# One fixed list of steps, laid out anew: the recurrent-attention and feed-forward kernel in another order

## The chip, the cores and the metric

The kernel runs on one core of a Trainium2 chip. The metric is the device time of one execution in microseconds (us). Three executions of the kernel before took 522.6, 523.03 and 520.49 us: median 522.6.

## What is computed

The reference runs a gated linear recurrence over 768 positions for 4 batches and 8 heads of width 48, and puts its output through a two-matrix feed-forward block with a squared ReLU.

```python
for t in range(S):                                   # S = 768, state is (B, H, D, D)
    cur = einsum('bhd,bhe->bhde', u * k[t], v[t])
    y[:, :, t] = einsum('bhd,bhde->bhe', r[t], state + cur)
    state = w[t][..., None] * state + einsum('bhd,bhe->bhde', k[t], v[t])
x = y.transpose(0, 2, 1, 3).reshape(3072, 384)
h = maximum(x @ w_in, 0)                             # w_in 384 x 2048
out = (h * h) @ w_out                                # w_out 2048 x 384
```

The two weight matrices come in 8-byte floats. Everything else is 4-byte.

## The kernel before

**Tiling.** The 768 positions are cut into 6 chunks of 128. For each chunk there are four attention units, one per batch (`attention`, lines 456 to 813), and then the feed-forward block on the chunk's 512 tokens (`ffn`, line 849). In chunk 0 the first six of sixteen feature blocks are done on batches 0 and 1 and then again on batches 2 and 3 (256 columns each); from the seventh on, 512 columns at once. Feature block pairs share a piece of weights, so there are 8 pieces of `w_in` (`ri`, `wi`) and 8 of `w_out` (`ro`, `wo`).

**A unit of chunk 0.** Six loads bring w, r and k of two batches (SP, line 471) and four more the v of one (line 504). PE transposes w, k and r (step "turn", line 518, four matmuls each). DVE scans w along time (line 535, four instructions), ScalarE takes Ln and Exp of it (lines 542 and 543), DVE makes the scaled k (lines 558, 559, 562). PE forms the scores ("mt", line 756), DVE masks them (759), PE mixes them with v (line 780, "mix" and "mix2") and makes the new state ("dS", line 790), which DVE scales (line 812). ACT and DVE move the result out as a high and a low part (lines 611 and 614). From chunk 1 on, the score, state and mixing matmuls of neighbouring units stand in one step (lines 650, 668, 677, 687).

**A feature block.** Nine matmuls into a PSUM bank `hp` ("hp", line 860; two banks), ReLU and square and a copy on ACT (lines 865, 867, 871), the low part on DVE ("g4", line 872), then per batch three matmuls into `ob` ("ob", line 878; four banks).

**Weights.** An 8-byte piece is made into two 4-byte parts by six steps: ACT (line 428), DVE (lines 432, 436, 441), ACT (448) and one subtraction on POOL (449).

**What sets the order.** Nothing is scheduled when the kernel is built. The 2,446 steps are made in a fixed way and numbered; the table `ORDER` says in which order they are issued, `PLACES` which buffer of its pool each of 549 tile lifetimes gets, and `FILLS` before which steps PE runs dummy matmuls. Every engine and the DMA queue of SP work in that order, each strictly one after the other:

```python
for n in order:                      # Plan.order, line 72
    s = self.steps[n]
    ...
        place = pool[places[self.slots[k]]] if places else ...
...
for s in self.order():               # Plan.run, line 91
    if self.filler and s.fill[0]:
        self.filler(*s.fill)
    s.fn()
...
for _ in range(count):               # fill, line 350
    T.matmul(to, ident, ident, is_transpose=True, ...)
```

A filler is one 128 x 128 transpose of the identity (line 351) into a part of a PSUM bank that nobody reads. It waits for nothing but its place in PE's order.

Of the kernel before, what the change touches and what calls it, by code (L numbers as in the profile page):

```python
# [96 lines left out]
class Names:  # L97
# [121 lines left out]
)  # L219
FILLS = {  # L220
    16: (2, 'ob', 1), 55: (6, 'ob', 3), 30: (3, 'ob', 1), 57: (4, 'ob', 1), 71: (2, 'ob', 0), 48: (5, 'ob', 1), 82: (3, 'ob', 3), 89: (5, 'ob', 1),
    145: (3, 'ob', 0), 144: (7, 'ob', 0), 127: (8, 'side', 0), 168: (4, 'side', 0),
}

# [794 lines left out]
```

## Time and profile before

| | |
|---|---|
| profiled execution | 521.4 us, span 519.7 us |
| median of three executions | 522.6 us |
| PE busy | 506.6 us, 97% of the span |
| VectorE (DVE) busy | 358.3 us, 69% |
| ScalarE (ACT) busy | 319.1 us, 61% |
| GpSimd (POOL) busy | 87.8 us, 17% |
| SP's DMA queue | 46.82 MB, 47.6% of 16 engines' span |
| granted TensorE clock, mean | 1.0 |

A share of busy time is a mean over stages with different limits, so the stages are read one by one. The span is what the profiler saw from the first to the last instruction; the time of the execution is 1.7 us more. A matmul's end is modelled, and matmuls overlap, so start times say more than durations.

### The profile page before, as it was taken

How to read it: one execution, taken by the hardware profiler on the slowest of the kernel's cores; microseconds unless marked ns; L12 is line 12 of the kernel's file. 1: busy time of each engine (PE TensorE's matmuls, PEld its weight loads, DVE VectorE, ACT ScalarE, POOL GpSimd, SP SyncE). 2: the span in 40 equal slices, each digit the busy share in tenths (PEclk: the TensorE clock that was granted, in tenths of full speed). 3: DMA queues.
4: the chain of work that ended last, by engine and by line, in shares of the span. 5: the costliest groups of instructions: out<-in, count | busy, mean ns of one | idle time of the engine just before them, and what ended most of it. 6: DMA issues, size and time to landing. Idle time of an engine off the chain costs nothing.

```text
span 519.7 us, 13752 instructions
## 1 busy us (share of the span) xinstructions
PE 506.6 (97%) x5452; PEld 458.5 (88%) x5452; DVE 358.3 (69%) x787; ACT 319.1 (61%) x878; POOL 87.8 (17%) x133
## 2 busy tenths in 40 slices
PE   8999999999999999999998999999999999999996
PEld 7888898888999998899987989889988888998895
DVE  6999789898687988768778658678476354333332
ACT  4999898996766867666573656564543363433232
POOL 3025233344021040212203001303000000000000
PEclk9999999999999999999999999999999999999999
DMA  7999977363847765575772480661181000100001
GB/s 152 225 165 247 246 151 205 88 92 63 148 71 100 147 97 95 106 125 73 117 129 37 84 137 15 112 122 36 32 133 32 3 19 6 59 16 0 1 2 65
DMA packets 188310, 48.74 MB, mean 94 GB/s; under 512 B 178000, under 2 KB 183120, under 8 KB 188240
## 3 DMA queue, kind: packets, MB, share of 16 engines
q1 hardware_dynamic: 187520, 46.82, 47.6%
q8 instruction: 45, 0.74, 0.6%
q10 hardware_dynamic: 720, 0.98, 0.5%
q14 instruction: 25, 0.20, 0.1%
HBM read 31.65 MB, written 4.72 MB: 70 GB/s over the span
## 4 chain that ended last, share of the span: by engine, by line
PE 78%; SPq 5%; issue 5%; DVE 4%; ACT 4%; DMA 2%; POOL 1%; POOLq 0%; ACTq 0%; DVEq 0%
PE ob L878 35%; PE hp L860 34%; PE ob L668 2%; SPq L504 2%; PE ob L687 2%; DMA ri<-in_moe_w_in_dram 2%; PE a L677 2%; SPq L415 1%; PE a L650 1%; PE hp L635 1%; SPq L471 1%; POOL wi L449 1%; DVE pt L535 1%; ACT t L865 1%; DVE m L550 1%
## 5 line engine op out<-in xcount | busy, mean ns | idle before, releaser
L878 PE MATMUL ob<-wo,g 128*128 128x384 f32 x1152 | 227.0, 340 | 0.1
L860 PE MATMUL hp<-x,wi 128*128 128x512 f32 (+1 forms) x1062 | 221.8, 355 | 3.2 <-DVE g L872 2.5
L878 PEld LDWEIGHTS ob<-wo,g 128*128 128x128 f32 x1152 | 199.4, 188 | 8.1 <-DVE g L872 0.9
L860 PEld LDWEIGHTS hp<-x,wi 128*128 128x128 f32 x1062 | 174.1, 188 | 29.7 <-DVE g L872 3.7
L869 DVE SCALAR_TENSOR_TENSOR hp<-hp,t 128x512 f32<-128x512 f32 (+1 forms) x96 | 58.2, 606 | 74.5 <-ACT t L865 74.2
L865 ACT ACTIVATE t<-hp 128x512 f32<-128x512 f32 (+1 forms) x118 | 61.0, 517 | 72.2 <-PE hp L860 47.7
L872 DVE TENSOR_TENSOR g<-hp,g 128x512 fp32r<-128x512 f32 (+1 forms) x118 | 69.1, 587 | 35.5 <-ACT g L871 35.0
L871 ACT CAST g<-hp 128x512 fp32r<-128x512 f32 (+1 forms) x118 | 59.6, 506 | 49.5 <-DVE hp L869 48.6
L630 ACT ACTIVATE m<-diag,beta 128x64 f32<-128x64 f32 x160 | 40.4, 338 | 3.4 <-DVE beta L593 3.3
L658 POOL MEMSET S<- 1x1 f32 x20 | 2.2, 110 | 237.4 <-PE ob L668 237.4
L614 DVE SCALAR_TENSOR_TENSOR x<-ob,x 112x128 fp32r<-112x128 f32 x80 | 21.2, 284 | 19.3 <-ACT x L611 16.5
L822 ACT COPY ob<-zero 112x128 f32<-112x128 f32 x80 | 20.7, 270 | 17.3 <-PE ob L878 10.1
L611 ACT ACTIVATE x<-ob 112x128 fp32r<-112x128 f32 x80 | 19.1, 275 | 17.3 <-PE ob L687 12.1
L535 DVE TENSOR_TENSOR_SCAN pt<-pt,zero 112x128 f32<-112x128 f32 x64 | 27.2, 456 | 2.4 <-DMA x<-x 1.1
L449 POOL TENSOR_TENSOR wi<-q,wi 128x768 fp32r<-128x768 f32 x8 | 17.1, 2135 | 55.1 <-ACT wi L448 44.0
L584 POOL TENSOR_TENSOR st<-st 128x384 f32<-128x384 f32 x16 | 16.7, 1043 | 33.0 <-DVE st L480 32.5
L480 DVE STREAM_TRANSPOSE st<-st 128x1152 f32<-128x1152 f32 x16 | 21.6, 1363 | 0.0
L542 ACT ACTIVATE m<-pt 112x512 f32<-112x512 f32 x24 | 15.1, 631 | 9.2 <-DVE pt L535 8.2
L449 POOL TENSOR_TENSOR wo<-q,wo 128x768 fp32r<-128x768 f32 x8 | 15.9, 1983 | 18.1 <-ACT wo L448 14.8
L558 DVE TENSOR_TENSOR pt<-pt,m 112x512 f32<-112x512 f32 x24 | 16.9, 706 | 2.4 <-ACT Ec L557 1.3
L559 DVE SCALAR_TENSOR_TENSOR m<-pt,m 112x512 f32<-112x512 f32 x24 | 18.0, 748 | 0.3
L709 DVE COPY_PREDICATED m<-caus,a 128x256 f32<-128x256 uint8 x40 | 17.3, 439 | 0.9 <-PE a L650 0.9
(125 smaller groups left out, 540.0 us busy)
## 6 DMA issues: line engine op xcount, KB each, us to landing
pt<-st SPq DMA_DIRECT2D x96, 96.0 KB, 2.9
ro<-in_moe_w_out_dram SPq DMA_DIRECT2D x8, 768.0 KB, 6.1
v<-in_v_dram SPq DMA_DIRECT2D x96, 48.0 KB, 2.8
out_dram<-q SPq DMA_DIRECT2D x20, 192.0 KB, 2.1
ri<-in_moe_w_in_dram SPq DMA_DIRECT2D x32, 96.0 KB, 4.9
ri<-in_moe_w_in_dram SPq DMA_DIRECT2D x8, 384.0 KB, 6.1
st<-in_r_dram SPq DMA_DIRECT2D x8, 384.0 KB, 5.3
st<-in_w_dram SPq DMA_DIRECT2D x8, 384.0 KB, 4.9
```

Source lines behind the costliest of these rows:

```text
L449: P.add("pool", 1.9, rank(8 * k + 5), lambda q=q, tt=tt: G.tensor_tensor(out=tt[:, 1], in0=q.tile, in1=tt[:, 0].bitcast(F32), op=ALU.subtr ...
L480: V.transpose(out=zt[:, i].rearrange("a t p q i -> a t (p q) i"), in_=sv[:, :, i].rearrange("s t p q x -> s t (p q) x"))
L535: lambda p=p: V.tensor_tensor_scan(out=pt[:, 0, p], data0=src(0)[:, p], data1=zero.broadcast_to([HP, C]), initial=1.0, op0=ALU.mult, op1=A ...
L614: made.append(P.add("dve", c2, rank(nm + "l"), lambda y=y, hi=hi, lo=lo: V.scalar_tensor_tensor(out=lo(), in0=y(), scalar=-1.0, in1=hi().b ...
L630: A.activation(M.tile[:, o:o + Q], diag2, AF.Copy, scale=beta.tile[:, i:i + 1])
L822: P.add("act", 0.16, rank("zero"), lambda p=p: A.copy(out=obs[p][0:HP, DM:], in_=zero[0:HP].broadcast_to([HP, C])), w=[("YO", p)], after=t ...
L860: T.matmul(hp.tile[:, 0:n], wi[f][:, wl, kt], xT[:, kt, xl, xs], start=(m == 0), stop=(m == 3 * KT - 1))
L865: P.add("act", 0.49 if full else 0.28, rank("g1"), lambda: A.activation(t(), h(), AF.Relu), r=[hp], w=[(g, 1)])
L869: P.add("dve", 0.605 if full else 0.337, rank("g2"), lambda: V.scalar_tensor_tensor(out=h(), in0=h(), scalar=0.0, in1=t(), op0=ALU.max, op ...
L871: P.add("act", 0.48 if full else 0.26, rank("g3"), lambda: A.copy(out=hi(), in_=h()), r=[hp], w=[(g, 0)])
L872: P.add("dve", 0.605 if full else 0.335, rank("g4"), lambda: V.tensor_tensor(out=lo(), in0=h(), in1=hi().bitcast(F32), op=ALU.subtract), r ...
L878: T.matmul(obs[b][:, 0:DM], g.tile[0][:, gl, o:o + C], wo[f][:, wl], start=(f == 0 and m == 0), stop=(f == NF - 1 and m == 2))
```

## The change

The steps, their instructions and their buffers' sizes stay. `ORDER`, `PLACES` and `FILLS` are replaced in part. Places 817 to 2445 of `ORDER` are as before; of the first 817, nearly all hold another step. On PE the last differing place is the 165th step of 593, "hp at 40.0", which the trace of before has at 148.6 us; from there on every engine has the same steps in the same order. There are 68 fillers in place of 52, before twelve steps as before, of which five are others.

```diff
 ORDER = (
-    4, 14, 17, 19, 6, 16, 0, 5, 20, 1, 18, 26, 15, 11, 7, 23, 24, 25, 55, 58, 309, 21, 22, 27, 28, 8, 2, 13, 30, 9, 57, 31, 312, 59, 33, 56, 64, 10, 29, 61,
...
+    4, 6, 14, 19, 20, 16, 11, 18, 51, 0, 1, 17, 5, 23, 12, 15, 9, 2, 26, 21, 22, 309, 7, 311, 310, 57, 8, 64, 312, 10, 24, 25, 27, 28, 30, 31, 32, 29, 33, 55,
...
 FILLS = {
-    16: (2, 'ob', 1), 55: (6, 'ob', 3), 30: (3, 'ob', 1), 57: (4, 'ob', 1), 71: (2, 'ob', 0), 48: (5, 'ob', 1), 82: (3, 'ob', 3), 89: (5, 'ob', 1),
-    145: (3, 'ob', 0), 144: (7, 'ob', 0), 127: (8, 'side', 0), 168: (4, 'side', 0),
+    16: (2, 'ob', 1), 1: (4, 'ob', 2), 15: (2, 'ob', 2), 57: (4, 'ob', 1), 56: (9, 'ob', 1), 71: (2, 'ob', 0), 48: (11, 'ob', 1), 89: (8, 'ob', 1),
+    144: (13, 'ob', 0), 127: (2, 'ob', 0), 473: (9, 'side', 0), 191: (2, 'side', 0),
 }
```

What this does to the engines is shown at three places. A line that begins with - stood there before, with + stands there now.

**The start.** In SP's queue, from the sixth transfer of before (the eighth now). `st_143` holds w, k and r of batches 0 and 1 of chunk 0, `v_91` the v of batch 0, `ri_56` the first piece of `w_in`:

```order
 L415 DMA ri_56<-in_moe_w_in_dram 48x512
-L471 DMA st_143<-in_k_dram 128x8x48
-L504 DMA v_91<-in_v_dram 64x4x48
-L471 DMA st_143<-in_r_dram 128x8x48
+L471 DMA st_143<-in_w_dram 128x8x48
 L415 DMA ri_56<-in_moe_w_in_dram 16x3x512
+L415 DMA ri_56<-in_moe_w_in_dram 48x512
+L471 DMA st_143<-in_k_dram 128x8x48
```

The k of batch 1 was the seventh transfer and is now the twelfth. On PE the same stretch, from the transpose of batch 0's k to that of batch 1's k; `ob_147` to `ob_150` are the four `ob` banks, `hp_151` and `hp_152` the two `hp` banks:

```order
+L351 MATMUL ob_149<-ident 128x128 x2
 L518 MATMUL ob_149<-ident,st_143 112x128 x4
-L351 MATMUL ob_150<-ident 128x128 x6
-L518 MATMUL ob_150<-ident,st_143 112x128 x4
-L351 MATMUL ob_148<-ident 128x128 x3
-L575 MATMUL ob_147<-ut,m_162 128x4 x4
 L351 MATMUL ob_148<-ident 128x128 x4
 L518 MATMUL hp_152<-ident,st_143 112x128 x4
+L575 MATMUL ob_147<-ut,m_163 128x4 x4
+L518 MATMUL ob_150<-ident,st_143 112x128 x4
+L351 MATMUL ob_148<-ident 128x128 x9
 L518 MATMUL hp_151<-ident,st_143 112x128 x4
```

Batch 1 is transposed in the order r, w, k in place of w, r, k, and nine fillers now stand ahead of its k. The step behind this piece is the scores of batch 0.

**The last batch of chunk 0.** On PE, the transposes of batch 3 (`st_144`) and the scores of batch 2 (L756, into `a_153` and `a_154`, the two PSUM banks of pool `a`):

```order
 L860 MATMUL hp_151<-x_142,wi_57 128x256 x9
-L351 MATMUL ob_147<-ident 128x128 x3
 L518 MATMUL a_154<-ident,st_144 112x128 x4
-L351 MATMUL ob_147<-ident 128x128 x7
+L351 MATMUL ob_147<-ident 128x128 x13
 L518 MATMUL ob_149<-ident,st_144 112x128 x4
-L518 MATMUL hp_152<-ident,st_143 112x128 x4
 L756 MATMUL a_153<-pt_136 64x128
```

The second feature block, which stood ahead of this piece, now stands behind the scores that begin at its last row, and so does the first transpose of chunk 1 (`st_143`). Thirteen fillers stand between the two transposes where there were seven, with three more ahead.

**Feature blocks and weights.** On DVE, the low parts of the last half-width block and of the first full-width one (L872, 128x256 and 128x512) among the steps on the weights (`q`, lines 432 to 441). Before:

```order
L872 TENSOR_TENSOR g_99<-hp_151,g_99 128x256
L436 SCALAR_TENSOR_TENSOR q_156<-ro_70,q_156 128x768
L812 TENSOR_TENSOR S_140<-a_154,Ec_172 112x96
L441 SCALAR_TENSOR_TENSOR q_156<-ro_70,q_156 128x768
L872 TENSOR_TENSOR g_95<-hp_152,g_95 128x512
```

Now:

```order
L436 SCALAR_TENSOR_TENSOR q_156<-ro_70,q_156 128x768
L441 SCALAR_TENSOR_TENSOR q_156<-ro_70,q_156 128x768
L872 TENSOR_TENSOR g_99<-hp_152,g_99 128x256
L558 TENSOR_TENSOR pt_135<-pt_135,m_166 112x512
L872 TENSOR_TENSOR g_95<-hp_151,g_95 128x512
```

Two weight operations stood between the two low parts and now stand ahead of both. In SP's queue of the same stretch a transfer of the seventh piece of `w_in` (`ri_80`), whose place holds v of chunk 0, has come ahead of the second halves of the sixth and fourth pieces (`ro_78`, `ro_70`):

```order
L415 DMA ri_80<-in_moe_w_in_dram 16x3x512
L504 DMA v_160<-in_v_dram 64x4x48
L417 DMA ro_78<-in_moe_w_out_dram 128x2x768
L417 DMA ro_70<-in_moe_w_out_dram 128x2x768
L415 DMA ri_76<-in_moe_w_in_dram 96x2x512
```

Before, `ro_70` went out ahead of every transfer of `ri_80`, and `ro_78` behind some of them.

## Rows read from the trace of the kernel before

**Rows 1.** The profile's page: busy us (share of the span) and instructions.

```profile
PE 506.6 (97%) x5452; PEld 458.5 (88%) x5452; DVE 358.3 (69%) x787; ACT 319.1 (61%) x878; POOL 87.8 (17%) x133
```

**Rows 2.** Busy by stretch: us, PE, PEld, DVE, ACT, POOL, PEclk, DMA share, GB/s.

```profile
5.58:57.00 51.42, 48.26 (x645) 42.88 (x645) 45.13 (x87) 44.16 (x124) 13.92 (x7) 1.00 0.94 210
33.00:57.00 24.00, 22.52 (x288) 19.94 (x285) 21.42 (x37) 22.12 (x59) 9.48 (x5) 1.00 0.93 223
57.00:80.00 23.00, 22.04 (x171) 20.56 (x171) 19.29 (x31) 20.78 (x49) 6.46 (x4) 1.00 0.88 186
80.00:150.00 70.00, 69.93 (x820) 63.02 (x819) 59.64 (x124) 59.02 (x165) 21.10 (x20) 1.00 0.58 116
150.00:300.00 150.00, 147.85 (x1906) 135.97 (x1905) 118.71 (x287) 95.96 (x295) 30.22 (x52) 1.00 0.60 99
```

**Rows 3.** PE in order of time: start, us, line, operation, [idle before].

```profile
12.96 0.90 PE L756 MATMUL a<-pt 64*64 64x128 f32 x32
...
31.66 0.93 PE L351 MATMUL ob<-ident 128*128 128x128 f32 x7
32.42 0.60 PE L518 MATMUL ob<-ident,st 128*112 128x128 f32 x4
...
33.39 0.90 PE L756 MATMUL a<-pt 64*64 64x128 f32 x32
...
53.31 0.65 PE L518 MATMUL hp<-ident,st 128*112 128x128 f32 x4 [0.87 <-DVE g L872]
...
57.56 1.35 PE L860 MATMUL hp<-x,wi 128*128 128x256 f32 x9
```

**Rows 4.** All fillers (line 351): count, ns least/mean/most, first and last start.

```profile
L351 PE MATMUL ob<-ident x52: 270/273/421, 6.4 to 47.3; 128*128 128x128 f32 x52
```

**Rows 5.** SP's queue: the twelfth transfer; landing times of line 471, 0 to 16 us.

```profile
9.92 0.60 SPq L471 DMA_DIRECT2D st<-in_w_dram  x1
...
DMA to landing us min/median/max: 3.2/4.2/5.0
```

**Rows 6.** DVE in order of time: scans, batch 2's scaled k, two weight operations.

```profile
26.71 0.73 DVE L535 TENSOR_TENSOR_SCAN pt<-ob,zero 112x128 f32<-112x128 f32 x2
...
30.90 0.26 DVE L812 TENSOR_TENSOR S<-a,Ec 112x96 f32<-112x96 f32 x1
31.07 0.69 DVE L562 TENSOR_TENSOR pt<-ob,m 112x512 f32<-112x512 f32 x1
...
49.46 0.96 DVE L436 SCALAR_TENSOR_TENSOR q<-ro,q 128x768 uint32<-128x768 uint32 x1
...
50.46 2.47 DVE L441 SCALAR_TENSOR_TENSOR q<-ro,q 128x768 uint32<-128x768 uint32 x1
```

**Rows 7.** Two subtractions on POOL in order of time; ACT's group of line 605.

```profile
39.91 2.70 POOL L449 TENSOR_TENSOR wi<-q,wi 128x768 fp32r<-128x768 f32 x1 [6.52 <-ACT wi L448]
...
49.75 2.36 POOL L449 TENSOR_TENSOR wo<-q,wo 128x768 fp32r<-128x768 f32 x1 [2.11 <-ACT wo L448]
...
L605 ACT ACTIVATE st<-st,nfar 128x384 f32<-128x384 f32 x24 | 14.8, 619 | 0.2
```

**Rows 8.** POOL, DVE and PE in order of time, 74 to 81 us.

```profile
74.78 1.84 POOL L449 TENSOR_TENSOR wi<-q,wi 128x768 fp32r<-128x768 f32 x1 [6.75 <-ACT wi L448]
74.94 2.49 DVE L436 SCALAR_TENSOR_TENSOR q<-ro,q 128x768 uint32<-128x768 uint32 x1
...
79.13 2.13 PE L860 MATMUL hp<-x,wi 128*128 128x512 f32 x8 [0.96 <-DVE g L872]
```

**Rows 9.** Whom PE waited for, 150 to 300 us: total, times, longest.

```profile
PE hp L860 <- DVE g L872: 1.5, 1, 1.5
```

**Rows 10.** Line 417's landing times; batch 3's state on PE; ACT's weight step.

```profile
DMA to landing us min/median/max: 4.8/6.1/10.1
...
56.95 0.67 PE L790 MATMUL a<-v,m 64*64 64x48 f32 x32
...
70.36 0.90 ACT L428 ACTIVATE q<-ro 128x768 f32<-128x768 f32 x1
```

92 rows, old and new, of tables (ORDER, PLACES) are left out of this document.

## The prediction

> **What bounds the kernel.** I read the profile's page first: PE is busy 506.6 of 519.7 us [rows 1]. Only two things can move the time much: PE's idle time, and work added to PE. No matmul of the computation is added or taken; fillers are. The busy times by stretch then say where the idle time lies [rows 2]. From the first transpose at 5.58 to 57 us PE is idle 51.42 − 48.26 = 3.16 us, from 57 to 80 us 0.96, from 80 to 150 us 0.07, from 150 to 300 us 2.15. The granted clock is 1.00 in each of these stretches, so the change has no clock to win back. The same rows show who limits PE early on: from 33 to 57 us DVE is busy 21.42 and ACT 22.12 of 24 us, so an operation moved ahead of a needed one on either delays that one by nearly its whole length. Then PE in order of time gives the landmarks [rows 3]: scores of batch 0 at 12.96, scores of batch 2 at 33.39, and at 57.56 the first feature block of the second pass. I compare the kernels at that last point, at equal PE work. Last I read the waits at each place where PE stood still [rows 3, 8, 9].
>
> **Fillers.** Seven of them stand between 31.66 and 32.42 [rows 3], 0.109 us each. There were 52 [rows 4], there are 68: 16 × 0.109 = 1.74 us more PE work, which always runs. It costs nothing where PE would have waited anyway, and all of it where it would not.
>
> **Term 1, start to 57 us: +0.45.**
> (a) The k of batch 1 goes from the seventh to the twelfth transfer of SP's queue, and on PE its transpose stands ahead of the scores of batch 0. The twelfth transfer was issued at 9.92, and this kind of load lands 3.2 us later at the least and 4.2 at the median [rows 5]: 13.1 to 14.1. I take the early end, since the transfers ahead of it change little in bytes; transpose at 13.3, scores of batch 0 at 13.7 in place of 12.96, +0.7. The nine fillers ahead of it (0.98 us) lie inside that wait.
> (b) On DVE the scaled k of batch 2 (31.07 [rows 6]) loses two operations ahead of it, a scan (0.73 for two, 0.37) and one scaling of the state (0.17, start to start): −0.5. The late start carries +0.4 to it, and the exp of batch 1 on ACT now stands behind a far pair that costs 0.5 of its 0.62 [rows 7]. Net: some 0.3 later.
> (c) On PE the scores of batch 2 lose ahead of them the second feature block (1.2 us by its sister's 1.35 [rows 3]) and one transpose, and get six more fillers. They start at about 32.8, not 33.39; but at equal work this is +1.1, of which the mix of batch 2, with four feature-block steps fewer of fillers and waits ahead, gets back nearly all: +0.2 at 38 us.
> (d) POOL's subtraction of piece 1 (39.91 [rows 7]) follows the DVE chain to about 40.55, and the third feature block waits for it: +0.9 at 44 us.
> (e) At 50.46 a weight operation on DVE took 2.47 us where its neighbour took 0.96 [rows 6], while POOL subtracted from 49.75 to 52.11 [rows 7]; the low part behind it was late and PE idle 0.87 us at 53.31 [rows 3]. In the new order ACT's copy that releases that subtraction stands behind a natural log and a far pair more (0.62 each, taking the log like the far pass [rows 7]), a short copy, and the late start of (d): some 2.2 us later, when the weight operation is over. The gap goes: −0.9, less what it hides, leaving the sum at +0.45.
> Bounds: at best all 3.16 us of idle time go and the fillers stay, −3.16 + 1.74 = −1.4. At worst k lands at its median (scores at 14.5, +1.5) and the seven fillers not ahead of it lie on the path (0.76): +2.3. I take a value between, nearer to none, since the gains and losses above are of one size.
>
> **Term 2, 57 to 80 us: −0.96.** PE's idle 0.96 at 79.13 waited for a low part on DVE [rows 8]. Between the two low parts stood two weight operations, one stretched to 2.49 beside a subtraction on POOL that began at 74.78. Both now stand ahead of both low parts, and PE has a feature block's `ob` matmuls to do meanwhile. Between 0 and −0.96; I take the whole, as nothing new stands between the low parts but one scaled k (0.69 by its kind [rows 6]).
>
> **Term 3, 80 to 150 us: 0.** There is no idle time to win [rows 2]. The mixing of chunk 1, batch 1 now has fewer feature blocks ahead of it, so it could wait. The nearest wait of that kind is 1.5 [rows 9]: 0 to +1.5, and I take 0, since the DVE work ahead of it is shorter than PE's.
>
> **Term 4, after 150 us: 0.** The order is the same on every engine. The 1.5 us wait [rows 9] may go with another phase, or a new one come of the size of the two early ones: −1.5 to +1.
>
> **Sum.** 0.45 − 0.96 = −0.5: 520.9 against the profiled execution's 521.4. The median of the runs, 522.6, stands 1.2 above that execution, so the forecast is **522.1 us**. A measurement of this kernel can tell about 0.5%, 2.6 us, from no change; this is no change.
>
> **The rivals.**
> *Faster: the early idle time goes.* Terms 1, 2 and 4 at their low ends: −1.4 − 0.96 − 1.5 = −3.9, 518.7. For it: 3.16 us of idle time before 57 us is what a better order could win [rows 2]. Against it: 1.74 of fillers must lie wholly in waits, while DVE and ACT are as full as before.
>
> *POOL stops DVE at another place.* Twice a weight operation on DVE ended 0.8 us after POOL's subtraction beside it: 50.46 + 2.47 = 52.93 against 52.11, and 77.43 against 76.62 [rows 6 to 8]. Its length then is set by POOL, not by itself. In the new order the subtraction of piece 2 falls upon a weight operation that stands ahead of the masks of batch 3; delayed by about 1.1 us, these carry it to PE: term 1 at +1.5 in place of 0.45, the sum at +0.6, 523.2. Against it: the masks have PE work of their own length ahead. The Trainium skill, "SBUF — State Buffer", section "SBUF: two separate sides", says that a DVE operation with two SBUF inputs and a GpSimd operation that reads SBUF take a shared port as an exclusive lock and that the loser fully blocks; by that rule every such pair that the order lays side by side costs the rest of the other, and the two rows above agree with it.
>
> *Slower: SP's queue stops behind the seventh piece.* A transfer of `ri_80`, whose place holds v of chunk 0, now stands ahead of the second halves `ro_78` and `ro_70`. The queue is in order, and this transfer waits for the last reader of that v, batch 3's state on PE: 56.95 before [rows 10], ending near 59.6 now with the feature blocks that are laid ahead of it. `ro_70` then goes out at about 61.3 and lands 6.1 to 10.1 us later [rows 10], 67.4 to 71.4, up to 74.9 if the transfer ahead of it (786 KB at 223 GB/s [rows 2], 3.5 us) is served first. ACT needs it at 70.36 [rows 10] and is in order too; from there each us late is a us of ACT, which has 23 − 20.78 = 2.2 us to spare [rows 2]. This decides from a landing at 72.6 on. At the late end it leaves 2.3 us, and term 2's gain is lost with it, since DVE's weight operations follow ACT's: 0.45 + 2.3 = +2.75, 525.4. Against it: at the median it lands in time.
>
> **How the numbers follow.** Forecast 0.52 (522.1, no change), POOL's stop 0.20 (523.2, no change), faster 0.14, the queue 0.14. Of the two outer cases some parts lie within: the range runs from terms 1 and 2 at their low ends with a wait of 0.9 gone behind (−3.3: 519.3) to term 1 at its worst with term 2 at nothing (+2.3: 524.9), and leaves out most of both, less than 2 in 10. Faster by over 0.5%: 0.14. Within 0.5%: 0.52 + 0.20 = 0.72. Slower: 0.14.
>
> **What would show it.** In the changed profile: scores of batch 0 at about 13.7 with PE waiting for the DMA of k ahead of them; scores of batch 2 at about 32.8; the second pass's first feature block at about 58.0; no wait on a low part near 79; fillers to about 47 us, 68 of them; ACT's step on `ro_70` near 70 with no DMA ahead of it. A DVE weight operation of over 1.5 us between 45 and 50 speaks for POOL's stop; ACT idle before `ro_70` for the queue; PE idle from 5.58 to 57 us under 1.5 us for the faster rival. The prediction is wrong if the time leaves the range, and its reasons are wrong if the equal-work delay at 57.56 is outside −1.4 to +2.3, or if anything after 150 us moves by more than 1.5.

## The result, and the profile after

The change made the kernel slower: 524.52 us (median of ten executions, 523.35 to 529.39) against 522.18 us, ratio 1.0054, 95% interval 1.0031 to 1.0078. Measured once more beside the experiments the ratio was 1.0056 (1.0034 to 1.0078). That is 2.9 us more. The forecast was 522.1 us, 0.5 less than the 522.6 that the kernel before then had as its median.

The first profiled execution of the change was the longest of its ten (529.39 us), so I read a second one (524.78 us, span 523.1) and say where I use the first. The page's busy times and the stretches of the second, in the columns of [rows 1] and [rows 2]:

```profile
PE 509.7 (97%) x5468; PEld 462.1 (88%) x5468; DVE 358.8 (69%) x787; ACT 319.8 (61%) x878; POOL 87.8 (17%) x133
```

```profile
5.28:57.00 51.72, 49.59 (x642) 44.15 (x643) 44.40 (x85) 42.15 (x120) 12.26 (x7) 0.97 0.96 198
33.00:57.00 24.00, 22.59 (x288) 20.02 (x287) 22.02 (x40) 21.54 (x59) 8.92 (x5) 1.00 1.01 207
57.00:80.00 23.00, 21.72 (x172) 20.13 (x171) 19.66 (x29) 19.71 (x48) 7.65 (x4) 1.00 0.81 199
80.00:150.00 70.00, 69.04 (x812) 62.72 (x811) 57.45 (x121) 60.09 (x160) 21.52 (x20) 1.00 0.63 121
150.00:300.00 150.00, 147.50 (x1913) 136.32 (x1912) 119.77 (x291) 96.55 (x302) 30.22 (x52) 1.00 0.57 95
```

PE is idle 51.72 − 49.59 = 2.13 us in the first stretch, where it was 3.16, and 1.28 from 57 to 80 us, where it was 0.96. The granted clock of the first stretch is 0.97 and was 1.00. Less idle time and yet later: the busy time itself has grown, by the added fillers and by a stretch at a lower clock, both read below. PE in order of time, and the fillers, answer to [rows 3] and [rows 4]:

```profile
13.62 0.90 PE L756 MATMUL a<-pt 64*64 64x128 f32 x32
...
34.27 1.16 PE L756 MATMUL a<-pt 64*64 64x128 f32 x32
...
55.94 0.65 PE L518 MATMUL hp<-ident,st 128*112 128x128 f32 x4 [0.94 <-DVE g L872]
...
L351 PE MATMUL ob<-ident x68: 270/273/421, 6.1 to 49.1; 128*128 128x128 f32 x68
```

The scores of batch 0 begin at 13.62, those of batch 2 at 34.27 (33.39 before, 32.8 forecast), and the 0.87 us wait that stood at 53.31 is there at 55.94 with 0.94.

**Comparing two orders.** The orders differ, so I compare at places where both have done the same PE steps, in whatever order: after the first 18, 45, 80 and 146 steps, and at the last (the 593rd). In the trace of before the next step starts there at 22.80, 53.31, 81.87, 136.21 and 514.49 us. How much later it starts in a profiled execution of each kernel, and the ratio of its time to before's:

| kernel | 18 | 45 | 80 | 146 | last | ratio (95%) |
|---|---|---|---|---|---|---|
| a1, the change | +2.7 | +2.6 | +3.5 | +3.2 | +3.3 | 1.0056 (1.0034 to 1.0078) |
| h1, the change to 57 us, then before | +2.8 | +2.0 | +2.6 | +3.1 | +3.2 | 1.0061 (1.0028 to 1.0095) |
| h2, before to 57 us, then the change | −0.5 | −0.2 | +1.9 | +1.5 | +2.0 | 1.0042 (1.0014 to 1.0069) |
| h3, before to 23 us, then the change | −0.3 | −0.2 | +0.6 | +0.4 | +0.6 | 1.0013 (0.9991 to 1.0034) |
| h4, the change to 23 us, then before | +2.7 | +7.8 | +7.9 | +7.9 | +8.1 | 1.0099 (1.0065 to 1.0132) |
| p1, the change, low parts moved | +2.1 | +0.5 | +1.3 | +1.1 | +1.9 | 1.0047 (1.0024 to 1.0070) |
| p2, before, low parts moved | −0.2 | −1.6 | −1.7 | −0.1 | −0.3 | 1.0013 (0.9994 to 1.0033) |
| h3p, h3 with low parts moved | −0.6 | +0.3 | +1.5 | +1.3 | +1.2 | 0.9992 (0.9973 to 1.0010) |
| f1, the change, 52 fillers | +0.8 | +2.1 | +2.9 | +2.7 | +2.9 | 1.0082 (1.0054 to 1.0109) |
| f2, before, 67 fillers | +0.4 | +0.2 | +0.2 | +0.3 | +0.6 | 1.0024 (1.0006 to 1.0041) |
| e1, the change, SP's start of before | +4.8 | +3.9 | +4.7 | +4.5 | +4.9 | 1.0066 (1.0041 to 1.0091) |
| e1late, the change, SP's rest of before | +2.8 | +1.8 | +2.7 | +8.3 | +10.2 | 1.0223 (1.0200 to 1.0247) |
| e4, before, SP's start of the change | +2.1 | +1.7 | +1.8 | +1.8 | +1.3 | 1.0077 (1.0047 to 1.0107) |
| e5, the change, k and v forward | +0.8 | +2.0 | +2.9 | +2.7 | +3.0 | 1.0050 (1.0024 to 1.0076) |
| e5p, e5 with low parts moved | +0.6 | −0.3 | +1.0 | +0.7 | +1.2 | 1.0038 (1.0014 to 1.0062) |
| b1, h2 with low parts moved | −0.2 | −1.7 | +1.1 | +0.6 | +2.7 | 1.0034 (1.0013 to 1.0055) |

The columns are one execution each, the ratio is of 5 to 12 executions against those of before on the same chip. Where the two disagree, the ratio decides. In its second profile the change loses 2.7 us in the first 18 steps and 0.9 between the 45th and the 80th.

The granted clock differs from one execution to the next in both kernels. Its mean over the span was 0.9961 in the eight executions of a1 and 0.9980 in the thirteen of before beside them. A rough estimate from these two: 0.0019 × 522 = 1.0 us of the 2.9 is a lower clock. It does not account for all: the one execution of the change that had a clock of 1.000 took 523.35 us, the four of before with 1.000 beside a1 took 521.03 to 521.60.

### The profile page after: what moved, and what is told of

Same layout as the page of the kernel before. It is cut to its first block, busy times and chain, and to the rows that moved or that the text cites. A ratio compares the mean times of both kernels' runs of the same rounds, so it can differ in the third digit from the quotient of the medians.

```text
span 527.7 us, 13772 instructions
## 1 busy us (share of the span) xinstructions
PE 510.2 (97%) x5468; PEld 462.6 (88%) x5468; DVE 358.1 (68%) x787; ACT 319.8 (61%) x878; POOL 87.9 (17%) x133
## 4 chain that ended last, share of the span: by engine, by line
PE 81%; DMA 5%; SPq 4%; DVE 4%; ACT 3%; issue 1%; POOL 0%; ACTq 0%; DVEq 0%; POOLq 0%
PE hp L860 36%; PE ob L878 35%; PE ob L668 2%; PE ob L687 2%; DMA ro<-in_moe_w_out_dram 2%; PE a L677 2%; DMA ri<-in_moe_w_in_dram 2%; SPq L471 2%; SPq L504 1%; SPq L415 1%; PE hp L635 1%; PE a L650 1%; DMA v<-in_v_dram 1%; DVE pt L535 1%; PE hp L518 1%
## 5 line engine op out<-in xcount | busy, mean ns | idle before, releaser
L872 DVE TENSOR_TENSOR g<-hp,g 128x512 fp32r<-128x512 f32 (+1 forms) x118 | 69.0, 586 | 41.4 <-ACT g L871 40.9
L449 POOL TENSOR_TENSOR wi<-q,wi 128x768 fp32r<-128x768 f32 x8 | 18.4, 2303 | 46.4 <-DMA st<-in_r_dram 23.3
L584 POOL TENSOR_TENSOR st<-st 128x384 f32<-128x384 f32 x16 | 16.7, 1045 | 33.4 <-DVE st L480 32.8
L449 POOL TENSOR_TENSOR wo<-q,wo 128x768 fp32r<-128x768 f32 x8 | 14.7, 1834 | 29.7 <-ACT wo L448 17.3
L559 DVE SCALAR_TENSOR_TENSOR m<-pt,m 112x512 f32<-112x512 f32 x24 | 19.1, 798 | 0.3
```

Of the source, the lines that this page charges most:

```text
L449: P.add("pool", 1.9, rank(8 * k + 5), lambda q=q, tt=tt: G.tensor_tensor(out=tt[:, 1], in0=q.tile, in1=tt[:, 0].bitcast(F32), op=ALU.subtr ...
L872: P.add("dve", 0.605 if full else 0.335, rank("g4"), lambda: V.tensor_tensor(out=lo(), in0=h(), in1=hi().bitcast(F32), op=ALU.subtract), r ...
```

## The experiments

The theories, as the expectations name them: S, later E and T, put the loss on the start (transfers that come late there); L on a late half of the third piece of `w_out`; F on the 16 fillers; P on POOL's subtractions that stretch weight operations ahead of low parts; O on the order on PE.

A step's number in `ORDER` says only in which place each engine has it, so the experiments take one engine's order from one kernel and another's from the other, or cut both at the same number of steps. Line numbers are those of the change.

**The change again, and its parts: queue and fillers.** a1 is the change itself.

> The changed kernel unchanged, with a second profiled execution. Theory S (SP's queue at the start): in the trace of the change the scores of batch 0 begin at 15.19 us, 2.23 later than before, since k of batch 1 landed at 14.56; so here again at 14.5 to 15.5, and a ratio of 1.004 to 1.007. Rival L (second half of the third piece of w_out): in that trace ACT waited 2.4 us for it at 52.8 and PE 2.0 for ACT, and the granted clock fell to 0.5 from 54 to 61 us; if the change as such does this, it is seen here again and the span is near 527. If the time is near 524, the clock stays 1.00 there and PE's wait at 52 us is under 1 us.

The ratio and the span came as for theory S. The fall of the clock from 54 us on and ACT's wait at 52 us were not seen here; the clock fell earlier, from 17.5 to 21 us (read below). But the scores of batch 0 began at 13.62, earlier than S wanted, and the 2 us were lost somewhat later: at the 18th step.

e1 and e1late give one part of SP's queue back:

```diff
 SP's transfers by step number, 1st to 15th (e1; to the 35th)
-4, 6, 11, 51, 5, 12, 9, 309, 7, 311, 310, 8, 312, 10, 92
+4, 6, 5, 11, 7, 309, 8, 13, 9, 312, 10, 92, 12, 308, 53
 SP's transfers, 49th to 56th (e1late; from the 36th on)
-384, 349, 282, 399, 364, 182, 362, 365
+349, 182, 183, 185, 365, 363, 382, 364
```

> The changed kernel with the first 35 transfers of SP's queue in the order of before; all engines as in the change. Theory S: k of batch 1 lands near 10.5, scores of batch 0 near 13.0, the time falls by about 2 us to a ratio against before of 0.999 to 1.002. Rival L: the later queue is untouched, so the ratio stays at 1.004 to 1.007. Rival F (16 more fillers, 16 x 0.109 = 1.74 us, on PE's path): also 1.003 to 1.006, as they are all still there.

> The changed kernel with SP's transfers from the 36th on in the order of before; the first 35 and all engines as in the change. Theory S: the delay at the start stays, ratio 1.004 to 1.007. Rival L: the second half of the third piece of w_out lands 2 to 4 us earlier, ACT's wait near 52 us goes, ratio 1.000 to 1.003. Rival F: 1.003 to 1.006.

Both missed. e1 has k of batch 1 early, but the change's PE wants r of batch 1 first, and the old queue brings r late: PE waited 2.92 us for it at 11.87. e1late lost 10 us, 5.6 of them between the 80th and the 146th step; there PE waited twice for a low part on DVE, 6.1 us in all. Neither half of the old queue does well under the new order of the engines. So theory S in the form "the old queue repairs it" is refuted.

f1 takes 16 fillers out:

```diff
-    15: (2, 'ob', 2), 48: (11, 'ob', 1), 89: (8, 'ob', 1), 144: (13, 'ob', 0),
+    48: (5, 'ob', 1), 89: (6, 'ob', 1), 144: (7, 'ob', 0),
```

> The changed kernel with 52 fillers in place of 68: 6 taken before the transpose of batch 3 near 33 us, 6 and 2 before two state matmuls, 2 at the start; the order is that of the change. Rival F: 1.74 us less, ratio 1.001 to 1.003. Theory S and rival L: the fillers lie in waits, at most 0.5 us less, ratio 1.003 to 1.007.

At the 18th step it is 1.9 us ahead of a1. By the 45th the gain is down to 0.5: PE waited 0.64 us for DVE at 31.68 and 0.84 for ACT at 51.06, neither of which a1 has, and at 36.53 it waited 1.06 us for w of chunk 1, where a1 waited 0.36. The ratio is no better than the change's, so theory F is not borne out: in the order of the change other waits take the place of the fillers. f2 adds 15 to the kernel before:

```diff
-    48: (5, 'ob', 1), 89: (5, 'ob', 1), 144: (7, 'ob', 0),
+    48: (11, 'ob', 1), 89: (8, 'ob', 1), 144: (13, 'ob', 0),
```

> The kernel before with 67 fillers: 6 more ahead of the first state matmuls of batch 0, 3 more ahead of those of batch 1, 6 more ahead of a transpose of batch 3 (the change's counts at these three steps). If fillers cost what they take: 15 x 0.109 = 1.64 us, less what lies in the wait of 1.02 at 31 us; PE's 41st step 0.6 to 1.6 us later, ratio 1.001 to 1.003. If the chains on DVE and ACT set the time at 53 us: the 46th step is within 0.4 us, ratio 0.999 to 1.001.

There they cost 0.0024 × 522 = 1.3 us of the 1.64 that they take, which fits fillers that cost. But the interval is 0.3 to 2.1 us, and the profiled execution shows only 0.6 at the end.

**Where along the time.** h1 and h2 cut the two orders at about 57 us, h3 and h4 at about 23 us:

```diff
 h3, PE's 3rd to 8th step (18 are as before; 55, 57, 56 transpose w, r, k of batch 1)
-1, 15, 57, 30, 55, 56
+1, 15, 55, 30, 57, 56
```

> The change up to about 57 us (first 80 PE steps, 86 DVE, 93 ACT, 62 SP, 7 POOL, and its fillers), the order of before from there on. Theory E (the early part costs): the early part of the second profile of the change was 2.4 us behind at its end, so ratio 1.004 to 1.006. Theory P (POOL's subtractions stop weight operations on DVE, and a low part behind them keeps PE waiting: 0.94 us at 55.9, 0.57 at 68.7 and 0.71 at 79.7 in the second profile of the change): the first of the three is here, the other two are not, but before's own at 79 us is; ratio 1.003 to 1.005.

> The order of before up to about 57 us, with its fillers, and the change's from there on. Theory E: nothing is lost early, ratio 0.999 to 1.001. Theory P: the waits of 0.57 and 0.71 us behind stretched weight operations come, in place of before's 0.96: +0.3 us, and up to +0.8 as the second profile of the change lost between 64 and 84 us, ratio 1.0005 to 1.002.

h1 came as expected of theory E, with 1.0061. h2 should have lost at most 0.2% by theory P and lost 0.42%. Both have a wait behind the seam that neither order has: PE waited 0.8 us at 61.51 (h1) and 0.7 at 59.35 (h2) for a low part ahead of a step of chunk 1 (line 575). Each mix is slower than before. Which part costs more they don't show: the two intervals overlap, and both ratios hold the wait of the seam.

> The start as before (first 18 PE steps with their fillers, 32 DVE, 28 ACT, 35 SP, 3 POOL: to about 23 us), the change from there on, 56 fillers in all. Three profiled executions of the change or its variants were 2.1 to 2.9 us behind before when 18 PE steps were done, and kept 2 to 3 of it. Theory E (the start costs, by its transfers and its fillers): 18 steps are done within 0.3 us of before, and the ratio falls to 1.0005 to 1.0025. Theory P (only the stretched weight operations cost): the loss returns at 50 to 55 us, where the chain on DVE and ACT sets the time whenever PE comes earlier: ratio 1.004 to 1.006.

> The start of the change (to about 23 us, with its fillers) and before's order from there on, 64 fillers. Theory E: 18 PE steps are done 1.5 to 2.9 us late and most of it stays: ratio 1.002 to 1.005. Theory P: what follows has its own slack, as before's waits at 31 (1.02), 53 (0.87) and 79 us (0.96) are waits for DVE that a late PE does not have: half or more is made up by 80 us, ratio 0.999 to 1.002.

h3 decides: with only the first 23 us undone the ratio falls from 1.0056 to 1.0013. So 0.43%, 2.2 us, of the loss goes with them (0.6 to 3.9 us, by the intervals of the two). The 0.13% that is left is not clear of noise, although h3 has the whole later part of the change. `PLACES` is no part of the loss: h3 has the table of the change, h1 and h4 have that of before. In h3 PE reaches the scores of batch 0 and the mix of batch 1 (line 780) about as before, where the scores began at 12.96 [rows 3] and the mix at 21.89. Before:

```profile
21.89 0.55 PE L780 MATMUL a<-m,v 64*48 64x128 f32 x8
```

h3:

```profile
13.13 0.90 PE L756 MATMUL a<-pt 64*64 64x128 f32 x32
...
21.59 0.55 PE L780 MATMUL a<-m,v 64*48 64x128 f32 x8
```

h4, the reverse, lost even more than the change. Its profiled execution shows a second way to lose, PE and a stretch of it:

```profile
37.60 1.07 PE L518 MATMUL hp<-ident,st 128*112 128x128 f32 x4 [2.57 <-DMA st<-in_w_dram]
...
38.00:46.00 8.00, 8.00 (x59) 7.44 (x58) 6.46 (x10) 2.91 (x9) 0.00 (x0) 0.50 1.02 272
```

PE waited 2.57 us for w of chunk 1, and then the granted clock stood at 0.50, the lower of its two levels (1.2 GHz), for eight us in which PE was never idle.

**What the start loses.** h1's first 57 us are the change itself, with the clock at 1.00 all the way. PE in order of time, and two transfers of SP's queue (k of batch 1, the last v of batch 1):

```profile
11.77 1.15 PE L351 MATMUL ob<-ident 128*128 128x128 f32 x9
13.97 0.65 PE L518 MATMUL hp<-ident,st 128*112 128x128 f32 x4 [1.05 <-DMA st<-in_k_dram]
14.55 0.90 PE L756 MATMUL a<-pt 64*64 64x128 f32 x32
...
20.53 1.42 PE L351 MATMUL ob<-ident 128*128 128x128 f32 x11
...
24.86 0.33 PE L780 MATMUL a<-m,v 64*48 64x64 f32 x4 [1.36 <-DMA v<-in_v_dram]
```

```profile
8.53 0.42 SPq L471 DMA_DIRECT2D st<-in_k_dram  x1
...
20.29 0.61 SPq L504 DMA_DIRECT2D v<-in_v_dram  x1
```

The nine fillers run out, PE waits 1.05 us for k, and later 1.36 for v. The last v of batch 1 is the 25th transfer of the change and was the 22nd; it was issued at 20.29 and landed at 24.82, before at 17.55 and 20.76. Between the two waits stand eleven fillers where five stood: 6 × 0.109 = 0.65 us. In the second profile of the change neither wait is in the list of what PE waited for. The same time goes another way there, PE and two stretches:

```profile
17.57 1.44 PE L797 MATMUL a<-ly,sel 112*128 112x128 f32 x6 [0.32 <-ACT ly L801]
...
16.00:17.50 1.50, 1.24 (x14) 0.91 (x13) 0.91 (x3) 1.43 (x5) 0.00 (x0) 1.00 1.06 188
17.50:21.00 3.50, 3.44 (x37) 3.19 (x41) 2.92 (x7) 2.17 (x9) 0.00 (x0) 0.54 0.47 94
```

From 17.5 to 21 us PE is busy nearly throughout at a granted clock of 0.54. After seven steps it was 0.9 us ahead of h1 (+0.7 against +1.6), at the 18th step it is level with it.

A third transfer among the first 35 comes later: w of chunk 1, 33rd before and 35th in the change. Before, it was issued at 25.82 and landed at 32.37; in a1 it was issued at 29.76 and landed at 37.80. Of ten profiled executions with the change's first 35 transfers, PE waited for it in seven: 0.36 (a1), 0.42 (the change's first), 0.75 (e4), 1.05 (e5p), 1.06 (f1), 1.31 (e5) and 2.57 us (h4). In the eight with before's it waited 0.2 us at most. So a kernel that is earlier at the 18th step can lose that lead here. No run moves this transfer alone.

e4 and e5 try the transfers alone:

```diff
 e5, SP's transfers 8th to 25th
-309, 7, 311, 310, 8, 312, 10, 92, 13, 308, 93, 94, 328, 53, 327, 52, 95, 54
+8, 309, 7, 311, 310, 312, 10, 92, 13, 308, 93, 94, 53, 52, 54, 328, 327, 95
```

> The kernel before with the first 35 transfers of SP's queue in the order of the change; all engines and fillers as before. Theory T (transfers): PE needs r and k of batches 0 and 1 as early as it did, they come later; 18 PE steps are done 1.5 to 4 us late, ratio 1.003 to 1.008. Theory O (the order on PE and its fillers cost, not the transfers): within 0.5 us at the 18th step, ratio 0.999 to 1.001.

> The changed kernel with two moves in SP's queue: k of batch 1 from the 12th to the 8th transfer, and the three last loads of v of batch 1 ahead of two pieces of w_in. Theory T: PE's waits for k (0.4 to 1.1 us in the profiles of the change and its variants) and v (0.3 to 1.4) go, the 19th PE step starts 0 to 1 us after before's 22.80 in place of 2.1 to 2.9, ratio 1.001 to 1.004. Theory O: 18 steps are still done 1.5 us late or more, ratio 1.004 to 1.006.

e4 came as for theory T: the change's first 35 transfers under before's engines cost 0.77%. In its profile PE waited 0.40 us for k and 1.77 for w in the first 11 us, and the granted clock stood at 0.50 from 13 to 16 us. The mean granted clock of its nine executions was 0.9918, of before's 31 beside them 0.9978; by these, a rough estimate is that 0.6% of the 0.77% is the lower clock. In e5 PE's waits for k and v of batch 1 are gone and the 18th step is 1.9 us earlier than in a1, as T said; the time is not shown to be better (1.0050). In its profile the gain is lost at 36.86, where PE waits 1.31 us for w of chunk 1, which the moves did not touch, and the clock falls to 0.50 from 38 to 40. So the two waits are named and can be taken out, but a transfer that is needed later, or the clock, takes the time back.

**Low parts behind stretched weight operations.** The second profile of the change, DVE, POOL and PE in order of time at three places:

```profile
52.91 1.83 POOL L449 TENSOR_TENSOR wo<-q,wo 128x768 fp32r<-128x768 f32 x1 [3.07 <-ACT wo L448]
52.99 2.57 DVE L441 SCALAR_TENSOR_TENSOR q<-ro,q 128x768 uint32<-128x768 uint32 x1
55.48 0.41 DVE L872 TENSOR_TENSOR g<-hp,g 128x256 fp32r<-128x256 f32 x1
...
65.09 2.44 POOL L449 TENSOR_TENSOR wi<-q,wi 128x768 fp32r<-128x768 f32 x1 [6.74 <-ACT wi L448]
66.70 1.65 DVE L441 SCALAR_TENSOR_TENSOR q<-ro,q 128x768 uint32<-128x768 uint32 x1
68.27 0.41 DVE L872 TENSOR_TENSOR g<-hp,g 128x256 fp32r<-128x256 f32 x1
68.74 1.34 PE L860 MATMUL hp<-x,wi 128*128 128x256 f32 x9 [0.57 <-DVE g L872]
...
76.47 2.02 POOL L449 TENSOR_TENSOR wi<-q,wi 128x768 fp32r<-128x768 f32 x1 [5.33 <-DMA ri<-in_moe_w_in_dram]
76.81 2.49 DVE L441 SCALAR_TENSOR_TENSOR q<-ro,q 128x768 uint32<-128x768 uint32 x1
79.22 0.41 DVE L872 TENSOR_TENSOR g<-hp,g 128x256 fp32r<-128x256 f32 x1
79.69 1.67 PE L860 MATMUL hp<-x,wi 128*128 128x512 f32 x6 [0.71 <-DVE g L872]
```

Each weight operation ends 0.81 or 0.82 us after POOL's subtraction beside it (52.91 + 1.83 = 54.74, 52.99 + 2.57 = 55.56). The low part is next on DVE, and PE waits for it: 0.94, 0.57 and 0.71 us. p1 moves the three low parts one place forward, p2 does so with two in the kernel before:

```diff
 L436 SCALAR_TENSOR_TENSOR q<-ro,q 128x768
+L872 TENSOR_TENSOR g<-hp,g
 L441 SCALAR_TENSOR_TENSOR q<-ro,q 128x768
-L872 TENSOR_TENSOR g<-hp,g
```

> The changed kernel with three low parts on DVE each one place earlier, ahead of the weight operation that POOL stretches (the low parts of blocks 4, 8 and 11). Theory P: the stretched operations stay long (1.6 to 2.6 us), but PE's waits of 0.94, 0.57 and 0.71 us at 56, 69 and 80 us go or shrink below 0.3; 1.2 to 2.2 us less, ratio against before 1.001 to 1.003. Theory E: those waits are cover for work that is late anyhow; at most 0.6 us less, ratio 1.0045 to 1.006.

> The kernel before with two low parts on DVE each one place earlier, ahead of a weight operation (blocks 4 and 12). Theory P: its PE waits of 0.87 us at 53.3 and 0.96 at 79.1 shrink below 0.3, 0.9 to 1.8 us less, ratio 0.9965 to 0.9985. Theory E says nothing of it; if the low parts were not what PE waited for, ratio 0.999 to 1.001.

In p1 these three waits are gone. PE and DVE around the first, and the stretch of the other two:

```profile
52.55 0.42 DVE L872 TENSOR_TENSOR g<-hp,g 128x256 fp32r<-128x256 f32 x1 [1.02 <-ACT g L871]
52.89 1.23 DVE L441 SCALAR_TENSOR_TENSOR q<-ro,q 128x768 uint32<-128x768 uint32 x1
53.77 0.60 PE L518 MATMUL hp<-ident,st 128*112 128x128 f32 x4
...
57.00:80.00 23.00, 22.74 (x173) 20.64 (x172) 16.42 (x28) 20.20 (x50) 8.19 (x4) 1.00 0.85 187
```

PE's idle time from 57 to 80 us falls from 1.28 to 0.26, and the 18 steps' loss of 2.1 is down to 0.5 at the 45th. But the ratio moved only from 1.0056 to 1.0047, with intervals of ±0.0023: the times alone don't show the gain. And the stretch ends just short of a new wait. DVE, ACT and PE of p1 in order of time:

```profile
75.86 0.42 DVE L872 TENSOR_TENSOR g<-hp,g 128x256 fp32r<-128x256 f32 x1 [1.45 <-ACT g L871]
76.20 0.95 DVE L441 SCALAR_TENSOR_TENSOR q<-ro,q 128x768 uint32<-128x768 uint32 x1
77.18 0.83 ACT L448 CAST wo<-q 128x768 fp32r<-128x768 f32 x1 [1.36 <-DVE q L441]
...
80.25 0.69 DVE L872 TENSOR_TENSOR g<-hp,g 128x512 fp32r<-128x512 f32 x1 [2.50 <-ACT g L871]
80.99 2.37 PE L860 MATMUL hp<-x,wi 128*128 128x512 f32 x9 [1.23 <-DVE g L872]
```

DVE stands idle 1.45 us for the low part that now comes first. The weight operation behind it, no longer stretched, begins at 76.20, ACT's copy waits 1.36 us for it, the steps of the next feature block stand behind that copy on ACT, and PE waits 1.23 us for that block's low part. So p1 loses 0.9 us between the 45th and the 80th step, as a1 does. h3p, e5p and b1 below have the same wait (1.22, 1.22 and 1.57 us) and lose 1.2, 1.3 and 2.7 there. Of the three moves only the first shows a gain in the profile.

In p2 the wait at the 45th step is gone as well: 1.62 us are won there and 1.65 at the 80th. They are given back by the 146th: at 81.12 PE has waited 0.57 us for the other end of the same chain, and the rest goes in smaller pieces.

```profile
PE ob L878 <- POOL wo L449: 0.6, 1, 0.6
```

The delayed weight operation is the one that lets ACT and POOL finish the second half of the fourth piece, and PE needs that piece next. p2 is no faster (1.0013; theory P wanted 0.9985 or less, and the interval begins at 0.9994): before's two waits were cover for this. Theory P's price for p2 is refuted.

h3p puts both together, e5p and b1 are two further mixes with the low parts moved:

> The same with the three low parts on DVE moved ahead of the stretched weight operations (blocks 4, 8 and 11) as well. Theory E with P: ratio 0.997 to 1.000, the waits at 55, 69 and 80 us gone and no loss at the start; PE's 165th step starts within 0.5 us of before's 147.59 or earlier. If the weights themselves are the next limit (in the kernel before with two low parts moved, 1.65 us of gain at 80 us were given back by 84): ratio 1.000 to 1.002.

> The same with the three low parts on DVE moved ahead of the stretched weight operations. Theory T with P: 1 us or so less than e5, ratio 0.998 to 1.002. Theory O: 1.002 to 1.005.

> The order of before up to about 57 us with its fillers, the change's from there on, and the three low parts on DVE moved ahead of weight operations (blocks 4, 8 and 11). The same without the three moves had a ratio of 1.0042 and was 2.0 us behind at the end in its profile, with waits of 0.8, 0.6 and 0.7 us behind the stretched operations. Theory P: 1 to 2 us less than that, ratio 0.998 to 1.002; if it is under 0.998, the later part of the change has a gain of its own. If the weights are the limit: ratio 1.002 to 1.004.

The ratio of h3p came out as for E with P, 0.9992 (0.9973 to 1.0010): with before's start and the three low parts moved the loss is gone, and nothing is won. But its profiled execution, the longest of its twelve, was 0.9 us behind at the 165th step, not level. h3 to h3p is 0.21%, within the ±0.28% of the two taken together: that the low parts cost time is not shown by it. e5p, at 1.0038, fits theory O; b1, at 1.0034, fits the weights as the limit: it was 0.2 us behind at the 165th step and 2.7 at the end, although the order is the same from there on. No version was faster than before.

## Why the prediction was right or wrong

The time, 524.52, lies in the range (519.3 to 524.9), near its upper end; the side was wrong. By the prediction's own sign its reasons failed too: the delay at equal work was to stay under +2.3 at 57.56 us, and it was +2.6 after the 45th step (53.31 us before) and +3.5 after the 80th (81.87). "Slower by over 0.5%" had 0.14, for another reason than the one that came true.

- **Term 1, +0.45: it was +2.6 (45th step, second profile).** Step (a) came near for k, with luck: it landed at 13.00 there and 13.93 in h1 (14.56 in the change's first profile), scores at 13.62 and 14.55 against a forecast of 13.1 to 14.1 and 13.7, the fillers inside the wait. But the twelfth transfer went out at 8.5 to 8.9 us, not at 9.92, and took 4.1 to 5.7 us, not 3.2; the two errors took each other away. The step that failed is what (a) left out. It priced one transfer of the moved ones. It left out the loads of v of batch 1, the last of which went from the 22nd place to the 25th; PE waited for it 0.8 to 1.4 us in four profiled executions (the change's first, h1, p1, h4). It left out w of chunk 1, which landed 5.4 us later in a1, and 0.65 us of fillers ahead of the state matmuls of batch 0. h3 shows the sum: 2.2 us of the loss go with the first 23 us. How it divides among transfers, fillers, PE's order and the clock stays open: e4 says the transfers alone are enough to lose that much, most of it by the estimate through the clock; e1 and e5, which give some of them back, do not repair it.
- **The clock.** The text read 1.00 in every stretch and took the clock for settled. That was a reading of one execution of before; the thirteen beside a1 had means from 0.995 to 1.000. With all or part of the new order the clock fell in the profiles of the change (17.5 to 21 us; in its first 54 to 61 us, behind a wait of 1.98), of e1, e1late, h4, e4 and e5. A term for this was missing altogether; the estimate above puts it at 1.0 us.
- **Steps (b) to (d)** came out about right in their sum, from +0.7 to +0.9 by forecast: between the 18th and the 41st step (before's transpose at 46.45) the change went from +2.67 to +2.80. No run tests them one by one.
- **Step (e), −0.9: it was −0.2** (41st to 45th step). "Some 2.2 us later, when the weight operation is over" moved POOL and left DVE where it was. Both moved: the subtraction from 49.75 to 52.91, the weight operation from 50.46 to 52.99, and the wait stayed, 0.94.
- **Term 2, −0.96: it was +0.9** (45th to 80th step). The wait at the first full-width block went as forecast. "Nothing new stands between the low parts" was true of those two and not the question: ahead of the low parts of blocks 8 and 11 stood weight operations that now met a subtraction, and PE waited 0.57 and 0.71 us, the second at 79.69, where the prediction wanted no wait. The step left out that the wait could come back at another low part. But these two waits are not the whole price of the stretch: in p1 and h3p they are gone, and it costs 0.9 and 1.2 us all the same, through the wait at 81 us that takes their place. What an order that wins here would need stays open. In the times, all that the change has behind its first 23 us (h3, 1.0013) is not clear of noise.
- **Terms 3 and 4, 0 and 0:** −0.3 from the 80th to the 146th step and +0.1 from there to the end. Right in the change; in p1 and b1 1.2 and 2.5 us moved from the 165th step on, where the orders are equal.
- **POOL's stop (0.20)** was the right mechanism at the wrong place. Its place was the masks of batch 3; there were three places, all low parts, at 56, 69 and 80 us. The first kept the 0.9 us that step (e) had counted as gone. By the rule of the Trainium skill ("SBUF — State Buffer", section "SBUF: two separate sides") every such pair costs the rest of the other; the five stretched pairs of the two kernels agree, each ending 0.81 or 0.82 us behind POOL. Applied to all weight operations in the new order, and not to the one in view, it would have named the two waits that term 2 left out.
- **The queue behind the seventh piece (0.14)** did not come. In the second profile ACT's step on `ro_70` ran at 73.89 and did not wait for a transfer. In the change's first profile ACT did wait 2.4 us at 52.8, for the second half of the third piece.

Sum in the second profile: 2.6 + 0.9 − 0.3 + 0.1 = 3.3, and the execution is 524.78 − 521.4 = 3.4 longer.

## What to carry to other kernels

When an order is changed, list every transfer that a near-future instruction needs with its old and new place, not only the one that moved most: the queue is served in order, and here five places cost k 1.9 to 2.3 us in its issue. Price a wait that is to go by what comes due next behind it; two kernels here lost their waits and not their time. And two operations that disturb each other must both be dated anew, since a delay ahead of them moves them together.

## What the runs showed of the hardware

- **Who waits, POOL or DVE.** When the weight operation on DVE wins, it takes its 0.95 us and POOL's subtraction ends 1.7 us after it (before, 39.97 + 0.95 = 40.92 against 39.91 + 2.70 = 42.61); when POOL wins, DVE ends 0.81 to 0.82 us after POOL. The recorded starts do not say who wins: with POOL's record 0.08 us ahead DVE was stopped (52.99), in the same profile with 0.60 ahead (a weight operation at 104.58) it was not.
- **The clock fell behind some short waits and not behind others.** It stood at or near 0.50 for 3 to 9 us behind PE waits of 0.32 (a1), 0.34 (e1late), 1.31 (e5), 1.77 (e4), 1.98 (the change's first profile), 2.57 (h4) and 2.92 us (e1). It did not fall behind waits of 1.23 (p1), 1.36 (h1) and 3.6 us (e1late, at 118.66). So the length of the wait alone does not decide it, and what does stays open. What follows a fall takes longer: the six matmuls of line 797 took 1.44 us at 17.57 in the second profile of the change and 0.91 at 16.28 in h3. The largest case is the change's first profile, PE and a stretch:

```profile
53.86 1.24 PE L797 MATMUL a<-ly,sel 112*128 112x128 f32 x6 [1.98 <-ACT ly L801]
...
54.00:61.00 7.00, 7.00 (x50) 6.61 (x51) 4.79 (x6) 4.60 (x12) 3.62 (x2) 0.52 0.96 236
```

This execution was 0.3 us behind a1 at the 41st step, 4.2 at the 80th and 4.6 at the last: that wait and the seven us behind it account for most of what it took beyond the others, 529.39 against 524.5.
